# Transposing the probabilities of a windowed attention 128 rows at a time

## The chip, the cores and the metric

The kernel runs on one core of one Trainium2 chip. The metric is the time of one execution on the device in microseconds (us), and the figure given for a kernel is the median of its runs.

## The reference

Two parts follow each other: an attention with a local window and block summaries, and a gated network without a nonlinearity.

```python
# q, k, v: 4 batches, 8 heads, 768 positions, 64 channels
k_sum = k.reshape(B, H, nb, 32, D).max(axis=3)      # nb = 24 blocks of 32
v_sum = v.reshape(B, H, nb, 32, D).mean(axis=3)
scores_l = scale * q @ k^T, kept where |i - j| < 16, else -1e9
scores_s = scale * q @ k_sum^T + log(32)
a = softmax(concat([scores_l, scores_s]))           # with 1e-9 added to the sum
attn = a @ concat([v, v_sum])
x = attn, heads side by side: 3072 tokens x 512
out = ((x @ w1) * (x @ w2)) @ w3 @ w_out            # 512 -> 1024 -> 1024 -> 512
```

## The kernel before

The tokens are cut into six groups of 512, and the heads are taken two at a time, so there are 24 *steps*: a step is one pair of heads for 512 tokens. Each group of 512 tokens is four blocks of 128, and each block has two halves of 64 rows. A half of 64 rows meets 96 positions of its window and 24 summaries, 120 columns in all (`KR`).

A step goes through these stages:

1. `begin` and `scores` (line 355): 32 products of 64 x 64 by 120 columns, for two heads, four blocks and two halves. Each product uses one quarter of TensorE's array: the head decides the rows, the half the columns. The scores of one head lie in one PSUM bank, the two halves of a block one above the other in its 128 partitions.
2. `reduce`, `expose`, `invert` and `normalize` (lines 364 to 402): VectorE adds the mask and takes the maximum, ScalarE takes the exponential and the sum, and the rows are divided by their sums. The probabilities of a step are the tile `sm`, 128 partitions by 8 by 120. The index `j` of the middle counts heads and blocks: `j = 4 * head + block`.
3. `transposes` (line 413): TensorE transposes the probabilities, since the next product needs the 120 columns on the partitions. Each transpose is a product with an identity as the moving operand and the probabilities as the weights. There are two PSUM banks, `tp[0]` and `tp[1]`, one for each half `g`.
4. `evacuate` (lines 418 to 422): one copy of each bank to SBUF, `pt[0]` and `pt[1]`. The first is ScalarE's, the second ScalarE's or VectorE's.
5. `outputs` (line 433): 32 products of 120 x 64 by 64 columns, probabilities times values. The head decides which 64 columns of the array are used.

Between these stages stand the products of the network. Line 123 (`products`) serves the folding of `w3` and `w_out` into one matrix (`w,w`) and the network of the first 1024 tokens (`x,w` and `wp,h`); line 708 (`lanes`) serves the network of the other 2048 tokens (`ln`), in a scheme with seven products in place of eight. Both take 128 x 128 weights and 512 columns, with operands rounded to f32r and split into a high and a low part, three products for one.

The order on TensorE's queue is written out by hand: `tc.manual_schedule` holds for SyncE and TensorE in the first loop, and for TensorE and GpSimd in the second. The first loop counts slots `t`. Steps 0 to 3 begin at slots 12, 18, 20 and 23 (`FIRST`), and the transposes of step `s` stand at slot `FIRST[s + 1]` (`first_pair`). Steps 4 and 5 are transposed together at the last of these slots (`four_pairs`), where step 4 uses the banks `tp` and step 5 the banks `sc` of the scores (`SPARE`). From then on `lump(p)` takes one step at a time: transposes of step `p - 2`, copies, scores of step `p`, eighteen or 24 products, outputs of step `p - 2`, and more products until the count `UP_TO[p]` is reached. For `p` of 24 and 25 there are no scores left, and products follow the transposes at once.

Of the kernel before, what the change touches and what calls it, by code (L numbers as in the profile page):

```python
# [19 lines left out]
P = 128  # L20
# [50 lines left out]
def attention_moe(ctx, tc, qG, kW, kT, vP, vW, vB, mask, w1, w2, w3T, wo, out, outT):  # L71
    nc = tc.nc
# [4 lines left out]
    NBLK = U // P  # L77
# [5 lines left out]
    KR = CUT + NB  # L83
# [16 lines left out]
    ident = const.tile([P, P], F32, name="ident")  # L100
# [305 lines left out]
    def transposes(sm, **more):  # L406

        tp = [ps.tile([P, 512], F32, name="tp", **more or {"bufs": 2}) for _ in range(2)]
        for j in range(NI):
            for g in range(2):  # L410
                rows = slice(64 * g, 64 * g + 64)
                to, p = tp[g][:KR, j * 64 : j * 64 + 64], sm[rows, j]
                nc.tensor.transpose(to, p, ident[rows, rows])  # L413
        return tp

    def evacuate(tp, second="V"):
# [8 lines left out]
    def outputs(pt, v, **more):  # L425

        po = ps.tile([P, 512], F32, name="po", **more or {"tag": "tp", "bufs": 2})
        for i in range(NBLK):
            for g in range(2):
                at = (2 * i + g) * 64  # L430
                for h in range(2):
                    cols = slice(h * D, (h + 1) * D)
                    nc.tensor.matmul(  # L433
                        po[cols, at : at + 64],
                        lhsT=v[:KR, g, i, cols],
                        rhs=pt[g][:, (h * NBLK + i) * 64 : (h * NBLK + i + 1) * 64],
                        start=True,
                        stop=True,
                    )
        return po  # L440
# [583 lines left out]
    def first_pair(s):  # L1024

        u, sm, mx, sc = begin(s)
        yield
        reduce(u, 0, sc, sm, mx)
        reduce(u, 1, sc, sm, mx)
        expose(0, sm, mx)  # L1030
        yield
        expose(1, sm, mx)
        invert(mx)
        yield
        normalize_alone(s, sm, mx)
        while t[0] < FIRST[s + 1]:
            yield
        pt = evacuate(transposes(sms.pop(s)[0], **(SPARE if BANKS[s] == "S" else {})), SECOND[s])
        yield
        keep_x(outputs(pt, values.pop(s)), xs[u])  # L1040
# [15 lines left out]
    def four_pairs(s):  # L1056

        steps = two_pairs(s)
        yield from steps
        while t[0] < FIRST[-1]:  # L1060
            yield
        steps = two_pairs(s + 2)
        tps = [transposes(sms.pop(p)[0], **more) for p, more in zip((s, s + 1), ({}, SPARE))]
        pts = [evacuate(tp, SECOND[p]) for p, tp in zip((s, s + 1), tps)]
        next(steps)
        for p, pt in zip((s, s + 1), pts):
            keep_x(outputs(pt, values.pop(p)), xs[place(p)[0]])
        yield
        yield from steps
# [128 lines left out]
    def finish_step(p, pt, **more):  # L1198
        u, c = place(p)
        po = outputs(pt, values.pop(p), **more)  # L1200
        if u < 2:
            keep_x(po, xs[u])
        else:
            keep_raw(po, u, c)
# [30 lines left out]
    def lump(p):  # L1235
# [8 lines left out]
        with tc.manual_schedule(engines={engines.Activation, engines.DVE}):  # L1244
            tp = transposes(sms.pop(p - 2)[0], **more)
            pt = evacuate(tp, 'V' if p in (12,13,) else 'A')
            b = begin(p) if p < NS else None
            if b:
                u, sm, mx, sc = b
                reduce(u, 0, sc, sm, mx)  # L1250
                if p > NFIRST + 1:
                    expose(0, sm, mx)
                    reduce(u, 1, sc, sm, mx)
# [91 lines left out]
```

## Time and profile before

| | us |
|---|---|
| median of 3 runs | 515.07 |
| lowest and highest run | 512.62 and 517.27 |
| the profiled execution, its own time | 512.96 |
| its span, first to last instruction | 511.2 |
| TensorE busy | 487.7 |
| transposes, union of their times (384 of them) | 16.4 |

Times in the profile are microseconds from the start of the span. PE is a product on TensorE and PEld the load of its weights, DVE is VectorE, ACT ScalarE, POOL GpSimd and SPq the queue of SyncE. A group of instructions is given by line, engine, operation, names (output<-inputs) and shapes; `64*120 64x64` is a product with 64 rows and 120 columns of weights and 64 moving columns. Products overlap in a pipeline, so the duration of one is longer than the distance to the next, and it is the distance between starts that fills the engine. The chain of waits follows the work that ended last back from the end of the span, and gives each piece its start and its length.

### The profile page before, as it was taken

How to read it: one execution, taken by the hardware profiler on the slowest of the kernel's cores; microseconds unless marked ns; L12 is line 12 of the kernel's file. 1: busy time of each engine (PE TensorE's matmuls, PEld its weight loads, DVE VectorE, ACT ScalarE, POOL GpSimd, SP SyncE). 2: the span in 40 equal slices, each digit the busy share in tenths (PEclk: the TensorE clock that was granted, in tenths of full speed). 3: DMA queues.
4: the chain of work that ended last, by engine and by line, in shares of the span. 5: the costliest groups of instructions: out<-in, count | busy, mean ns of one | idle time of the engine just before them, and what ended most of it. 6: DMA issues, size and time to landing. Idle time of an engine off the chain costs nothing.

```text
span 511.2 us, 10373 instructions
## 1 busy us (share of the span) xinstructions
PE 487.7 (95%) x3744; PEld 392.1 (77%) x3744; DVE 365.1 (71%) x883; ACT 314.2 (61%) x879; POOL 46.9 (9%) x86
## 2 busy tenths in 40 slices
PE   0989987999999999999999999999999999999996
PEld 0767766888887877777777887877787888888885
DVE  4979987688833598985459795899978029129972
ACT  5588964468635788878797677657875421423710
POOL 1024433011201210000000000000000000000000
PEclk9999997999999999999999999999999999999999
DMA  8996699999299989889987999998677755655762
GB/s 342 414 375 244 259 305 321 359 398 412 82 286 306 272 283 281 260 254 339 334 302 251 311 311 333 338 327 252 210 247 247 240 179 192 206 174 197 211 200 85
DMA packets 57220, 139.82 MB, mean 274 GB/s; under 512 B 6224, under 2 KB 19024, under 8 KB 54608
## 3 DMA queue, kind: packets, MB, share of 16 engines
q1 hardware_dynamic: 54864, 134.95, 77.5%
q0 software_dynamic: 1152, 2.10, 2.5%
q10 hardware_dynamic: 1152, 2.10, 1.1%
q8 instruction: 30, 0.49, 0.4%
q14 instruction: 22, 0.18, 0.1%
HBM read 106.42 MB, written 32.70 MB: 272 GB/s over the span
## 4 chain that ended last, share of the span: by engine, by line
PE 83%; DVE 5%; DMA 5%; ACT 5%; issue 1%; SPq 0%; ACTq 0%
PE ln L708 46%; PE mm L123 27%; PE po L433 5%; PE sc L355 4%; PE tp L413 2%; DMA rows<-in_vP_dram 2%; ACT sm L383 2%; DVE wf L186 2%; DMA v<-in_vW_dram 2%; DMA wraw<-in_wo_dram 1%; ACT wf L174 1%; ACT w L200 1%; DVE wf L183 1%; DVE w L119 1%; DVE ks L246 1%
## 5 line engine op out<-in xcount | busy, mean ns | idle before, releaser
L708 PE MATMUL ln<-xT,ws 128*128 128x512 f32 x672 | 157.1, 392 | 0.0
L708 PEld LDWEIGHTS ln<-xT,ws 128*128 128x128 f32 x672 | 125.0, 188 | 27.6 <-issue 0.8
L123 PE MATMUL mm<-x,w 128*128 128x512 f32 x384 | 92.5, 399 | 0.0
L123 PEld LDWEIGHTS mm<-x,w 128*128 128x128 f32 x384 | 72.7, 192 | 16.4 <-issue 0.8
L383 ACT ACTIVATE sm<-sm,mx 128x120 f32<-128x120 f32 x192 | 73.9, 389 | 9.3 <-DVE mx L369 9.3
L708 PE MATMUL ln<-hT,ws 128*128 128x512 f32 x336 | 78.3, 392 | 0.0
L728 DVE TENSOR_TENSOR tmp<-ln,tmp 128x512 f32<-128x512 f32 x52 | 35.8, 688 | 56.3 <-PE ln L708 42.1
L708 PEld LDWEIGHTS ln<-hT,ws 128*128 128x128 f32 x336 | 62.6, 188 | 13.4 <-issue 0.2
L123 PE MATMUL mm<-w,w 128*128 128x512 f32 x192 | 50.2, 414 | 14.3 <-ACT w L200 11.9
L619 ACT CAST hT<-hr 128x512 fp32r<-128x512 f32 x56 | 32.1, 622 | 42.6 <-DVE hr L785 35.4
L123 PEld LDWEIGHTS mm<-w,w 128*128 128x128 f32 x192 | 36.8, 197 | 24.7 <-ACT w L200 12.1
L369 DVE CUSTOM_DVE_ANT_0 sm<-sc,mask_sb 128x120 f32<-128x120 f32 x192 | 42.2, 276 | 15.1 <-PE sc L355 15.0
L123 PE MATMUL mm<-wp,h 128*128 128x512 f32 x192 | 46.3, 395 | 0.0
L393 ACT ACTIVATE sm<-sm,mx 128x120 f32<-128x120 f32 x128 | 38.9, 387 | 6.1 <-DVE mx L389 6.1
L123 PEld LDWEIGHTS mm<-wp,h 128*128 128x128 f32 x192 | 35.4, 188 | 8.0 <-issue 0.5
L119 DVE TENSOR_TENSOR hT<-hr,hT 128x512 fp32r<-128x512 f32 x56 | 35.5, 684 | 3.2 <-ACT hT L619 3.0
L383 ACT ACTIVATION_READ_ACCUMULATOR sm<-sm,mx 128x1 f32 x192 | 36.8, 192 | 0.0
L342 POOL COPY k<-ks 128x96 f32<-128x96 f32 (+1 forms) x32 | 12.9, 412 | 218.3 <-DMA k<-in_kW_dram 178.4
L433 PEld LDWEIGHTS po<-pt,v 120*64 120x64 f32 x768 | 25.2, 141 | 9.2 <-issue 5.0
L200 ACT CAST w<-wf 128x1024 fp32r<-128x1024 f32 (+1 forms) x22 | 21.3, 967 | 14.0 <-DVE wf L186 14.0
L433 PE MATMUL po<-pt,v 120*64 120x64 f32 x768 | 28.7, 229 | 1.1 <-DMA v<-in_vW_dram 0.6
L174 ACT ACTIVATE wf<-wraw 128x1024 f32<-128x1024 f32 (+1 forms) x22 | 23.1, 1056 | 8.0 <-DMA wraw<-in_wo_dram 3.6
(60 smaller groups left out, 548.5 us busy)
## 6 DMA issues: line engine op xcount, KB each, us to landing
ws<-wS SPq DMA_DIRECT2D x56, 512.0 KB
wraw<-in_w3T_dram SPq DMA_DIRECT2D x8, 1024.0 KB
wraw<-in_w_dram SPq DMA_DIRECT2D x8, 1024.0 KB
wS<-sp SPq DMA_DIRECT2D x16, 512.0 KB
ws<-pS SPq DMA_DIRECT2D x16, 512.0 KB
k<-in_kW_dram SPq DMA_DIRECT2D x20, 368.0 KB
raw<-in_kT_dram SPq DMA_DIRECT2D x16, 392.0 KB
q<-in_qG_dram SPq DMA_DIRECT2D x24, 256.0 KB
```

Source lines behind the costliest of these rows:

```text
L119: eng.tensor_tensor(dst, src, hi.bitcast(F32), ALU.subtract)
L123: nc.tensor.matmul(acc, lhsT=a, rhs=b, start=first and i == 0, stop=last and i == len(terms) - 1)
L174: nc.scalar.activation(f[:, some], words[:, some, 1].bitcast(F32), AF.Prelu, scale=2.0**-112, alpha=-(2.0**32),)
L200: nc.scalar.copy(t[:, 0, some], f[:, some])
L355: nc.tensor.matmul(sc[h][64 * g : 64 * g + 64, i * KR : (i + 1) * KR], lhsT=q[rows, i * P + 64 * g : i * P + 64 * g + 64], rhs=k[rows, i, ...
L369: nc.vector.tensor_tensor_reduce(out=sm[:, j], in0=sc[h][:, i * KR : (i + 1) * KR], in1=mask_sb[:, 0 if blk == 0 else 2 if blk == BLOCKS - ...
L383: nc.scalar.activation(sm[:, j], sm[:, j], AF.Exp, bias=mx[:, 0, j : j + 1], scale=-1.0, accum_out=mx[:, 1, j : j + 1])
L393: nc.scalar.activation(sm[:, j], sm[:, j], AF.Copy, scale=mx[:, 2, j : j + 1])
L433: nc.tensor.matmul(po[cols, at : at + 64], lhsT=v[:KR, g, i, cols], rhs=pt[g][:, (h * NBLK + i) * 64 : (h * NBLK + i + 1) * 64], start=Tru ...
L619: nc.scalar.copy(dst[0], src)
L708: nc.tensor.matmul(banks[i][:, :U], lhsT=x, rhs=y, start=c + j == 0 and k in o.first, stop=c == steps - 1 and j == 2 and k in o.last, skip ...
L728: nc.vector.tensor_tensor(parts[to], got, parts[more], ALU.add)
```

## The change

In `transposes` the inner loop over the halves `g` goes. One transpose takes all 128 partitions of `sm[:, j]` with the whole 128 x 128 identity as the moving operand, and writes 128 columns. The bank is now chosen by the head (`j // NBLK`) and the place in it by the block. So a bank holds one head with the blocks and halves in order of the tokens, where it held one half with heads and blocks. In `outputs` the moving operand is taken from the bank of the head `h`, at the same place `at` at which the result is written.

```diff
         tp = [ps.tile([P, 512], F32, name="tp", **more or {"bufs": 2}) for _ in range(2)]
         for j in range(NI):
-            for g in range(2):
-                rows = slice(64 * g, 64 * g + 64)
-                to, p = tp[g][:KR, j * 64 : j * 64 + 64], sm[rows, j]
-                nc.tensor.transpose(to, p, ident[rows, rows])
+            nc.tensor.transpose(tp[j // NBLK][:KR, j % NBLK * P : (j % NBLK + 1) * P], sm[:, j], ident)
         return tp
...
                     nc.tensor.matmul(
                         po[cols, at : at + 64],
                         lhsT=v[:KR, g, i, cols],
-                        rhs=pt[g][:, (h * NBLK + i) * 64 : (h * NBLK + i + 1) * 64],
+                        rhs=pt[h][:, at : at + 64],
                         start=True,
                         stop=True,
                     )
```

## The prediction

> **What bounds the kernel now.** I read the page's header first, then busy time by stage, then the chain of waits, and last single bursts of transposes in order of time.
>
> ```profile
> span 511.2 us, 10373 instructions
> ...
> PE 487.7 (95%) x3744; PEld 392.1 (77%) x3744; DVE 365.1 (71%) x883; ACT 314.2 (61%) x879; POOL 46.9 (9%) x86
> ```
>
> TensorE is busy for 95% of the span. The share is an average, so the stages decide (per row: stretch, its length, busy us and count of PE, PEld, DVE, ACT, POOL, then clock, DMA share, GB/s):
>
> ```profile
> 84.00:250.00 166.00, 165.99 (x1432) 133.83 (x1432) 116.52 (x341) 113.56 (x363) 19.18 (x35) 0.99 0.91 297
> 250.00:386.00 136.00, 136.00 (x1176) 108.81 (x1169) 109.42 (x289) 100.35 (x307) 2.30 (x10) 1.00 0.88 290
> ```
>
> From 84 to 386 us TensorE has no gap at all and its clock is full: every nanosecond that its stream grows or shrinks there moves the end. The chain of waits says the same and gives the pieces (start, us, what):
>
> ```profile
> 133.13 1.09 PE tp L413 x32
> 134.21 1.17 PE sc L355 x34
> ...
> 136.43 2.02 PE po L433 x64
> ...
> 146.83 0.20 PE tp L413
> ...
> 156.10 0.61 PE tp L413 x13
> ...
> 202.71 0.61 PE tp L413 x16
> 203.32 0.98 PE sc L355 x32
> 204.30 4.35 PE mm L123 x18
> 208.65 1.08 PE po L433 x32
> ...
> 281.09 8.38 PE ln L708 x36
> ...
> 349.74 0.61 PE tp L413 x16
> ...
> 365.15 0.61 PE tp L413 x16
> 365.76 4.33 PE ln L708 x18
> ...
> 379.55 0.61 PE tp L413 x16
> ...
> 385.57 121.46 PE ln L708 x534
> ```
>
> A step is one pair of heads for 512 tokens; there are 24. Each has one burst of sixteen transposes (line 413), and twenty of these bursts lie on the chain: a double one at 133 (two steps), one split into 1 and 15 at 147 and 156, fifteen from 162 to 350 that stand between products and scores like the one at 202.71, and two at 365 and 380 that stand between products and products. The other four come before 84 us.
>
> **The change, part by part.** It removes 16 transposes of 64 rows a step and adds 8 of 128 rows. No copy, DMA or bank is added, and the SyncE and GpSimd queues are not touched. So the price is the TensorE time of a burst before and after, taken from these rows.
>
> *Spacing now.* Thirty-two transposes take 1.09 us, sixteen 0.61, so eight pairs cost 0.48: 0.060 a pair. The two halves of a pair sit in different rows of the array and run together. That is visible in single slices (count of transposes in flight):
>
> ```profile
> 202.72:202.74 0.02, 0.02 (x2) 1.00 2.00 819
> 202.74:202.76 0.02, 0.02 (x4) 1.00 0.00 0
> ...
> 202.80:202.82 0.02, 0.02 (x6) 1.00 0.50 205
> ```
>
> They arrive by twos. So "half as many instructions" is no halving: sixteen now cost eight time slots.
>
> *What a burst costs besides.* In order of time:
>
> ```profile
> 202.32 0.39 PE L123 MATMUL mm<-x,w 128*128 128x512 f32 x1
> 202.64 0.68 PE L413 MATMUL tp<-ident,sm 64*120 64x64 f32 x16
> ```
>
> From the last product to the first transpose it is 0.32 us, while products follow each other every 121.46/534 = 0.2275. Entering the burst thus costs 0.09. The second pair comes at 202.75, 0.11 behind the first in place of 0.06: 0.05 for a first weight load that nothing covers. Of the burst's 0.61, 0.48 is spacing and 0.05 that load, so 0.08 is for leaving it. Entering products after a burst costs 0.10: 36 of them take 8.38, which is 0.19 over 36 x 0.2275, of which 0.09 is for leaving.
>
> *Spacing of the wide transpose.* No row shows it. Its stream is 128 columns of f32 in place of 64, and it has the array to itself. The nearest rows are these:
>
> ```profile
> L413 PE MATMUL tp<-ident,sm 64*120 64x64 f32 x384 | 16.4, 225 | 1.7 <-POOL sm L402 1.7
> ...
> L280 PE MATMUL means<-rows,mean_sb 128*24 128x128 f32 x48 | 1.5, 274 | 0.0
> ```
>
> ```profile
> 30.95 1.51 PE L280 MATMUL means<-rows,mean_sb 128*24 128x128 f32 x48
> ```
>
> Line 280 streams 128 f32 columns through all 128 rows, four side by side in different columns of the array: 48 take 1.51 us, less the last one's 0.274, over 11 gaps: 0.11 a group of four. That is the lower end. The upper end is today's transpose with its stream doubled, 2 x 0.060 = 0.12: same operation, same 120 columns of weights. I take 0.12, because it is the same operation and because line 280's weights are much narrower. The gain from running two halves at once is exactly what is lost: eight slots of 0.060 become eight of 0.12.
>
> What comes back is the change of shape. Products use 128 rows and 128 columns of the array, the wide transpose the same rows and 120 columns, so I take the 0.09 for entering and the 0.05 of uncovered load as gone. Leaving towards scores (64 x 64) stays at 0.08.
>
> *Sum.* Single step: from the last product to the first score, now 0.32 + 0.61 = 0.93; after, 0.2275 + 8 x 0.12 + 0.08 = 1.27. That is +0.34, fifteen times: +5.1.
> Double step: 0.32 + 1.09 = 1.41 becomes 0.2275 + 16 x 0.12 + 0.08 = 2.23, +0.82. Part of it returns:
>
> ```profile
> 134.73 0.61 ACT L420 COPY pt<-tp 120x512 f32<-120x512 f32 x1
> ...
> 135.39 0.81 PEld L355 LDWEIGHTS sc<-k,q 64*64 64x64 f32 x30 [0.24 <-ACT pt L420]
> ```
>
> The second scores wait 0.24 for the copy that empties their bank. After the change the first of each two banks is full halfway, so three of four copies start before the burst ends and the last needs 0.6 of the 0.98 that the first scores take; the wait goes. +0.58.
> Split step: its lone transpose costs 0.32 + 0.20 + (0.2275 + 0.10) = 0.85 up to the second product, after 0.2275 + 0.12 + 0.2275 = 0.58: -0.27. The other seven: 0.2275 + 7 x 0.12 + 0.08 - 0.93 = +0.22. Together -0.05.
> The two late steps: 0.32 + 0.61 + 0.10 = 1.03 becomes 0.2275 + 0.96 = 1.19, +0.16 each, +0.3.
> Total 5.1 + 0.58 - 0.05 + 0.3 = +5.9, say 6.0 us. With 0.11 a transpose, 160 of them on the chain take 1.6 less: +4.4.
>
> *Parts costed at nothing.* The four early steps lie where other work ends last:
>
> ```profile
> 74.37 8.38 DMA v<-in_vW_dram
> ```
>
> ```profile
> 76.92 0.69 PE L413 MATMUL tp<-ident,sm 64*120 64x64 f32 x16 [1.72 <-POOL sm L402]
> ...
> 81.09 0.64 PE L355 MATMUL sc<-k,q 64*64 64x120 f32 x16 [2.09 <-POOL k L342]
> ```
>
> The chain reaches 82.7 through VectorE, ScalarE and this load, and TensorE idles 2.09 us for a GpSimd copy behind the last of the four bursts. Without that cover they cost 4 x 0.34 = 1.4. The outputs now need the first copy for one head and the second for the other, so their first product needs both. Behind them stand 0.98 of scores and 4.35 of products, against two copies of 0.6: nobody waits. No wait is added.
>
> The profiled execution took 512.96 us with its span of 511.2; the runs shown have their median at 515.07. I add the 6.0 to the median: 521.
>
> **A rule against the sum.** Line 280 moves 128 f32 columns in 0.11 us, while products of 512 columns come every 0.2275: a quarter of the columns in half the time, so plain f32 costs about two passes. The Trainium skill, "FP8 and Floating Point Precision", section "TensorE Precision Notes", says that true FP32 takes four passes, by which the sum would be the third rival's, 538; the row speaks against four.
>
> **The rivals.**
>
> *The array is emptied anyway* (0.22). The products are rounded f32 and the transposes plain f32 in a transposing mode; if that change of mode, and not the tile, costs the 0.09, 0.05 and 0.10, they stay. Every change of shape around the products is also one of type, so the rows can't exclude it. Single: 0.32 + 0.05 + 0.96 + 0.08 = 1.41, +0.48, x15 = 7.2; double 2.37 - 1.41 - 0.24 = +0.7; split about +0.4; late +0.48 each. +9.3: 524.4. [...]
>
> *The weights set the pace* (0.12), the other side. If 0.060 is the load of 120 columns and not the stream of 64, a wide transpose with the same 120 also takes 0.060. Then a single step is 0.2275 + 0.48 + 0.08 = 0.79, -0.14, x15 = -2.1; double -0.14 - 0.24; split -0.5; late -0.33 each. -3.6: 511.5, no slower. The point from which it decides: a single step breaks even at (0.93 - 0.31)/8 = 0.077 a transpose. Against it: outputs stream 64 columns too, with 64 columns of weights, and 32 more of them, sixteen pairs, cost 2.02 - 1.08 = 0.94, 0.059 a pair. With half the weights the pace is the same.
>
> *Four passes when the array isn't shared* (0.05). Then 128 columns stand like a product's 512, 0.2275 a transpose: 160 x 0.1075 = 17 more, +23: 538. For it: every f32 row is of a shared array. Against: 0.11 for four of line 280 together.
>
> *Nothing reaches the end* (0.03), because TensorE's stretch has slack that the rows hide: 515. Against: 165.99 of 166.00.
>
> **How the numbers follow.** The forecast holds 0.58: +4.4 to +6.0, 519.5 to 521. About 1% (5.2 us) is what can be told from no change here. Of the forecast's 0.58 some 0.4 lies above it, since 0.12 is likelier than 0.11; with 0.22 and 0.05 this is 0.66 for slower. Within 1%: the rest of the forecast 0.17, the weights 0.11, nothing 0.03: 0.31. Faster by over 1% needs -5.2, past the second rival's sum: 0.03. The range takes in forecast and first rival and leaves out the weights and the four passes: 517 (519.5 less the 2 us by which the runs shown differ from their median) to 527.
>
> **What would show it.** Line 413 with 192 transposes of 128x128; eight filling about 0.96 us of starts; bursts on the chain of about 1.0; 0.23 from the last product to the first transpose (0.32 would be the first rival); spacing 0.06 the second, 0.23 the third; no wait for the copy L420 at the double step; the same 0.2275 in the last stretch. I am wrong if the spacing of eight is under 0.08, or if a new wait stands ahead of scores or outputs.

## The result

The changed kernel takes 518.92 us (median; 516.57 to 524.41) against 514.58 for the kernel before on the same occasions: a ratio of 1.008, 95% interval 1.0055 to 1.0104. That is slower by 4.3 us: less than the 1% that the prediction took as the bound of what can be told apart, but the interval is clear of 1. The ratio leaves out the one slow run, 524.41. The profiled execution took 518.46 us with a span of 516.7.

The profile after, its header and busy time:

```profile
span 516.7 us, 9978 instructions
...
PE 492.6 (95%) x3552; PEld 400.9 (78%) x3552; DVE 365.7 (71%) x883; ACT 313.9 (61%) x879; POOL 44.7 (9%) x86
```

192 TensorE instructions fewer, and 4.9 us more of TensorE. The group of the transposes, and the one wait of TensorE that the profile has between 86 and 391 us:

```profile
L410 PE MATMUL tp<-ident,sm 128*120 128x128 f32 x192 | 24.8, 272 | 0.0
```

```profile
PE ln L705 <- DVE xT L119: 0.8, 1, 0.8
```

The chain of waits of the changed kernel (start, us, what), beside the rows shown of before:

```profile
133.69 1.75 PE tp L410 x16
135.44 1.80 PE sc L355 x64
137.24 2.02 PE po L430 x64
...
204.24 0.87 PE tp L410 x8
205.11 0.98 PE sc L355 x32
206.09 4.30 PE mm L123 x18
210.40 1.08 PE po L430 x32
...
370.49 0.88 PE tp L410 x8
371.36 4.11 PE ln L705 x18
...
391.00 121.41 PE ln L705 x534
```

A single step's burst went from 0.61 to 0.87. At the double step the burst went from 1.09 to 1.75, and the scores behind it from 1.17 + 1.04 = 2.21 to 1.80. The last stretch of products is as it was. The spacing shows in slices of 20 ns (count of transposes in flight):

```profile
204.08:204.10 0.02, 0.02 (x1) 1.00 0.17 26
204.18:204.20 0.02, 0.02 (x2) 1.00 1.01 205
204.28:204.30 0.02, 0.02 (x3) 1.00 0.33 51
```

One arrives at a time, where two did. The trace's starts are 0.108 to 0.110 apart in every burst, the first gap included, and the first transpose of a burst starts 0.230 after the last product where it was 0.319.

One thing that the kernel's description ahead of the prediction has wrong: scores and outputs are sixteen products a step in the code, not 32. The profile records two instructions for each. That matters below.

### The profile page after: what moved, and what is told of

Its sections match the earlier page's. It is cut to its first block, busy times and chain, and to the rows that moved or that the text cites. A ratio compares the mean times of both kernels' runs of the same rounds, so it can differ in the third digit from the quotient of the medians.

```text
span 516.7 us, 9978 instructions
## 1 busy us (share of the span) xinstructions
PE 492.6 (95%) x3552; PEld 400.9 (78%) x3552; DVE 365.7 (71%) x883; ACT 313.9 (61%) x879; POOL 44.7 (9%) x86
## 4 chain that ended last, share of the span: by engine, by line
PE 80%; DVE 9%; DMA 6%; ACT 2%; issue 1%; SPq 1%; ACTq 0%
PE ln L705 43%; PE mm L123 26%; PE po L430 4%; PE sc L355 3%; PE tp L410 3%; DMA rows<-in_vP_dram 2%; DVE wf L186 2%; DMA v<-in_vW_dram 2%; DVE w L119 2%; DVE sm L369 1%; DMA wraw<-in_wo_dram 1%; DMA wS<-sp 1%; DVE wf L183 1%; DVE wp L119 1%; DVE ks L246 1%
## 5 line engine op out<-in xcount | busy, mean ns | idle before, releaser
L355 PE MATMUL sc<-k,q 64*64 64x120 f32 x768 | 25.2, 270 | 4.5 <-POOL k L342 4.5
```

The source lines that it names most:

```text
L355: nc.tensor.matmul(sc[h][64 * g : 64 * g + 64, i * KR : (i + 1) * KR], lhsT=q[rows, i * P + 64 * g : i * P + 64 * g + 64], rhs=k[rows, i, ...
```

## The experiments

Each is a kernel of its own, timed against the kernel before on the same chip unless said otherwise.

**Every wide burst twice.**

```diff
-        for j in range(NI):
+        for j in (*range(NI), *range(NI)):
             nc.tensor.transpose(tp[j // NBLK][:KR, j % NBLK * P : (j % NBLK + 1) * P], sm[:, j], ident)
```

> Every burst of eight wide transposes is issued twice (the second writes the same places again). Theory: TensorE's stream is the bound from 84 us on and each wide transpose costs 0.109 us there: 160 more on the chain add 17.4 us to the changed kernel's 518.9, 536.3 us, ratio to before 1.042, and a burst that stands between products and scores takes 15 x 0.109 = 1.64 us from first to last start. Rival: part of a burst is hidden behind other work's waits: under 530 us, ratio under 1.03.

Measured: 534.74 us, ratio 1.0403 (1.0365 to 1.0441). The chain:

```profile
197.80 1.75 PE tp L410 x16
199.55 0.98 PE sc L355 x32
...
210.90 1.75 PE tp L410 x16
```

Each burst grew from 0.87 to 1.75, so eight more cost 0.88, which is 0.11 each; the starts in the trace stand 0.109 apart. The stretch from the last outputs ahead of the long products to the last outputs of all took 321.6 us, 15.8 more than the changed kernel's 305.8, and the medians differ by 15.8 as well. Most of the 1.6 that is missing from the expected 17.4 stands in the two traces: a stall of 0.84 that is gone, and three products fewer at half clock, 0.2 each. So a transpose more lengthens this stretch by nearly its whole spacing.

**Ordinary products in place of the transposing mode.**

```diff
-            nc.tensor.transpose(tp[j // NBLK][:KR, j % NBLK * P : (j % NBLK + 1) * P], sm[:, j], ident)
+            to = tp[j // NBLK][:KR, j % NBLK * P : (j % NBLK + 1) * P]
+            nc.tensor.matmul(to, lhsT=sm[:, j], rhs=ident, start=True, stop=True)
```

> The wide transposes are issued as ordinary f32 products with the identity, no transposing mode; shapes and count are those of the changed kernel. Theory: the stream of 128 f32 columns sets the spacing of 0.109 and the mode has no part in it: 0.11 again, the entry stays at 0.23, and the time at 518 to 520 us, ratio to before 1.007 to 1.010. Rival: the ordinary load of 120 columns (0.1 us, as the first two loads of a product run stand 0.107 apart) can't be covered by a stream as short as it is: 0.2 a transpose, 160 x 0.09 = 14 us more, 533 us, ratio 1.036.

Measured: 533.34 us, ratio 1.0363 (1.0328 to 1.0399). The time is the rival's, the reason is neither. The groups by shape (count, busy us, mean ns):

```profile
L411 PE MATMUL tp<-ident,sm 128*120 128x128 f32 x384 | 45.9, 273 | 0.0
```

The code asks for 192 products and the profile has 384 instructions. Their starts stand 0.109 apart, from the first gap of a burst on, and each product takes two of them. An ordinary f32 product of 128 columns costs 0.218, the transposing mode half of that.

**The same with 64 moving columns at a time.**

```diff
-            nc.tensor.transpose(tp[j // NBLK][:KR, j % NBLK * P : (j % NBLK + 1) * P], sm[:, j], ident)
+            for g in range(2):
+                at = j % NBLK * P + 64 * g
+                to = tp[j // NBLK][:KR, at : at + 64]
+                nc.tensor.matmul(to, lhsT=sm[:, j], rhs=ident[:, 64 * g : 64 * g + 64], start=True, stop=True)
```

> Sixteen ordinary f32 products a step with 128 rows and 120 columns of weights and 64 moving columns, so the stream of each is half as long and each set of weights is loaded twice. Theory: if the stream sets the pace even at 64 columns, 0.055 to 0.06 each, 320 on the chain are 320 x 0.058 - 160 x 0.109 = +1.1 us on the changed kernel: 520 us, ratio 1.010. Rival: the load sets a floor of about 0.1: 320 x 0.105 - 17.4 = +16 us, 535 us, ratio 1.040.

Measured: 567.66 us, ratio 1.1039 (1.1001 to 1.1077).

```profile
205.78 3.31 PE tp L413 x32
209.09 0.98 PE sc L355 x32
```

Thirty-two instructions a burst, since each product is two, at 0.105: 640 more of them on the chain than the changed kernel's 160 make up 640 x 0.105 - 160 x 0.109 = 49.8, and the medians differ by 48.7. With half the stream the spacing hardly fell, from 0.109 to 0.105. The trace tells why: the first gap of a burst is 0.055, the others 0.103 to 0.105, and behind the second one the loads of the weights stand as far apart. The first two loads start with the product ahead of the burst and with the first transpose. So 64 columns take 0.055 where the weights are there in time, and otherwise the ordinary load of 120 columns sets a floor of 0.105. The expectation's rival had that floor, and missed the doubling. By the 0.055, an estimate for 128 columns is 0.11: the 0.109 of the ordinary products above is then the stream, though it lies close to the floor of the load. The transposing mode does not show that floor: the kernel before loads 120 columns of two row halves every 0.059.

**Wide transposes of rounded operands.** Results of the mask addition, the exponential and the division are written as f32r, so the probabilities lose low bits. Of the edit, the identity and the transposes are shown.

```diff
-    ident = const.tile([P, P], F32, name="ident")
+    ident = const.tile([P, P], F32R, name="ident")
...
-            nc.tensor.transpose(tp[j // NBLK][:KR, j % NBLK * P : (j % NBLK + 1) * P], sm[:, j], ident)
+            to = tp[j // NBLK][:KR, j % NBLK * P : (j % NBLK + 1) * P]
+            nc.tensor.transpose(to.bitcast(F32R), sm[:, j].bitcast(F32R), ident)
```

> The wide transposes take f32r operands: the mask addition, the exponential and the division round their results in sm to f32r, which changes the probabilities in their low bits; the shapes and the count are those of the changed kernel. Theory: the spacing of 0.109 is the stream of 128 plain f32 columns at two passes; f32r takes one (512 columns in 0.2275, so 128 in 0.057 or a little more): spacing 0.06, 160 x 0.049 = 7.8 us less than the changed kernel, 511.1 us, ratio to before 0.993, faster than both. Rival: the load of 120 columns of weights sets the pace, about 0.1 us as the first two loads of a product run stand 0.107 apart: spacing stays at 0.10 to 0.11 and the time at 518 to 519, ratio 1.007 to 1.009.

Measured: 515.04 us, ratio 1.0019 (0.9994 to 1.0043): between the theory and its rival.

```profile
L413 PE MATMUL tp<-ident,sm 128*120 128x128 f32 x192 | 18.6, 240 | 1.4 <-POOL sm L404 1.4
```

```profile
201.13 0.61 PE tp L413 x8
201.74 0.98 PE sc L357 x32
```

The same shape at the same clock fills 18.6 us where plain f32 filled 24.8, so plain f32 is what sets 0.109. That it is the stream and not the load shows at the first gap of a burst: the second load starts with the first transpose in both kernels, and the gap is 0.108 with plain f32 and 0.059 with f32r. But the spacing fell to 0.06 only at first: the starts of the burst at 201 us are 59, 61, 88, 76, 78, 80 and 86 ns apart, 75 on average. The trace has the loads of the weights 79 to 84 ns apart behind the second one. So the stream takes the expected 0.06 where the weights are there in time, and then the transposes follow the loads; why a load takes 0.08 here was not separated. A burst then costs what two narrow halves cost, 0.61. The prediction's point of break-even, 0.077 a transpose, is tried here: at 0.075 the time can't be told from that of the kernel before. The profiled execution has 2.0 us of waits of TensorE for ScalarE after 356 us, so the time bears this out only roughly.

**Only the early steps, only the late steps.** The wide transposes and their layout are used for steps 0 to 3 alone, or for steps 4 to 23 alone. `WIDE(s)` says whether step `s` is one of them; `outputs` chooses its operand by the same test.

```diff
         for j in range(NI):
-            nc.tensor.transpose(tp[j // NBLK][:KR, j % NBLK * P : (j % NBLK + 1) * P], sm[:, j], ident)
+            if WIDE(s):
+                nc.tensor.transpose(tp[j // NBLK][:KR, j % NBLK * P : (j % NBLK + 1) * P], sm[:, j], ident)
+            else:
+                for g in range(2):
+                    rows = slice(64 * g, 64 * g + 64)
+                    nc.tensor.transpose(tp[g][:KR, j * 64 : j * 64 + 64], sm[rows, j], ident[rows, rows])
```

> Only steps 0 to 3 transpose 128 rows at a time; steps 4 to 23 keep the row halves. Theory: the four early bursts lie under VectorE, ScalarE and the load of v, and cost the end nothing: 514.6 us, ratio 1.000 within 0.002, and the last outputs ahead of the long product stretch start at 82.8 us as before. Rival: the 0.7 us by which that place was later in the changed kernel's profile (83.55 for 82.83) is the early bursts' doing, since ScalarE's and VectorE's order there is planned anew: 515.3 us, ratio 1.0014, and the place at 83.5.

Measured: 516.72 us, ratio 1.0051 (1.0023 to 1.008).

> Only steps 4 to 23 transpose 128 rows at a time; steps 0 to 3 keep the row halves. Theory: the whole cost is here, 160 transposes at 0.109 us in place of 160 pairs at 0.059, less what the entries give back: +4.4 us, 519.0 us, ratio 1.0085, and from the outputs at 82.8 us on every piece as in the changed kernel. Rival: part of the cost is the early steps', and this one gains 0.7 us on the changed kernel: 518.2, ratio 1.007.

Measured: 516.57 us, ratio 1.0032 (1.0003 to 1.0061).

Neither theory. By the ratios the early four cost 2.6 us and the late twenty 1.6, less than their TensorE time, with intervals that overlap. The traces don't bear the first out: in the early kernel's trace the last outputs ahead of the long stretch start at 84.5, between the kernel before's 84.3 and the changed kernel's 85.0. So two more profiles were taken.

**Both kernels again.**

> The kernel before again, for a second profile of it. Theory of a late stall: TensorE's stretch from 86 to 386 us, without a gap in the profile shown, has gaps of 1 to 2 us in other executions, because ScalarE and VectorE behind it are near their limit, and a longer TensorE stream takes these up; this profile then shows such gaps. Rival: the stretch is always full and the profile shows none, and what differs between executions lies before 86 us and in the slices of half clock there. Either way the ratio is 1.000 within 0.003.

> The changed kernel again, on the same chip as the other runs of this study: ratio 1.008 within 0.003, and from the last outputs before the long product stretch to the last outputs of all 303.5 to 304 us when slow clock and gaps are taken off, 3.6 to 4.0 more than the kernel before.

Measured: 515.12 us, ratio 0.999 (0.9958 to 1.0022), and 518.64 us, ratio 1.0085 (1.0057 to 1.0113). TensorE's waits in the late stretch of the kernel before's second profile (in all, times, longest):

```profile
PE po L433 <- ACT pt L418: 0.9, 2, 0.5
PE ln L708 <- DVE xT L119: 0.4, 1, 0.4
PE ln L708 <- DVE tmp L728: 0.2, 1, 0.2
PE po L433 <- ACT pt L420: 0.2, 1, 0.2
```

The first profile has none. So the stretch that the prediction read as always full is full in some executions. In this one TensorE waits near 256 and 266 us for copies of ScalarE, 1.1 us by these rows, and near 274 and 276 us for VectorE, 0.6; shorter gaps bring the sum to 1.9. The chain behind the first of them:

```profile
244.10 10.38 DMA q<-in_qG_dram
...
254.49 0.02 ACTq L532
...
254.55 0.34 ACTq L532
```

Line 532 is the store of an output tile, issued from ScalarE's own queue. ScalarE is idle for 3.69 us there, and the profile puts that down to a load of `q` that landed 10.38 us after its issue; why the store waits for it the profile doesn't say. What ScalarE has to do behind the store, the copies of the transposes among it, starts late. In the first profile the same store goes out while ScalarE is still busy.

**A filler that keeps the clock up.** In the first profiles of both kernels TensorE idles before 82 us, and the clock granted then is half for 6.8 us, in which the first products of the long stretch fall. Twelve products of the identity with itself, overwritten later, were put where the scores of step 5 wait.

```diff
         for i in range(NBLK):
+            for _ in range(filler if i == 2 else 0):
+                nc.tensor.matmul(sc[1][:, 2 * KR : 2 * KR + P], lhsT=ident, rhs=ident, start=True, stop=True)
...
-        return u, sm, mx, scores(*inputs.pop(s))
+        return u, sm, mx, scores(*inputs.pop(s), 12 if s == 5 else 0)
```

> The kernel before, with twelve products of the identity with itself, whose result is overwritten, at the place near 79 us where TensorE waits for a GpSimd copy. Theory: that idle time ends in 3.4 to 10.2 us of half clock from about 82 us on, which costs the first products of the long stretch 0.2 us each; filling it keeps the clock up: 1.0 to 1.5 us less, 513.5 us, ratio 0.9975, slow clock per run down by half or more, and less spread. Rival: the wait behind it sets the end and the clock is beside the point, or the filler delays the scores: 514.9 to 515.5, ratio 1.000 to 1.001.

> The changed kernel with the same twelve products at the same place, where its idle time was 3.3 and 4.5 us in its two profiles. Theory: 1.0 to 2.0 us less than the changed kernel, 517.3 us, ratio to before 1.005; the distance to the kernel before with the filler is then the cost on TensorE's stream alone, 2.9 to 4.1. Rival, as with the kernel before: 518.9, ratio 1.008.

> Only steps 4 to 23 transpose 128 rows at a time, with the filler. Theory: with the clock kept up the early bursts make no difference, so this equals the changed kernel with the filler within 0.7 us: 517.3, ratio 1.005. Rival: the early bursts cost 1.7 to 2.6 us by themselves, as the runs with only the early or only the late steps changed gave: 515.2, ratio 1.001.

> Only steps 0 to 3 transpose 128 rows at a time, with the filler. Theory: equals the kernel before with the filler within 0.7 us: 513.5, ratio 0.9975. Rival: 1.7 to 2.6 us above that one: 515.5, ratio 1.0015.

| with the filler | median us | ratio to before |
|---|---|---|
| kernel before | 512.81 | 0.9998 (0.9972 to 1.0023) |
| changed kernel | 517.01 | 1.0051 (1.0022 to 1.0080) |
| only late steps wide | 515.93 | 1.0011 (0.9983 to 1.0039) |
| only early steps wide | 515.43 | 1.0000 (0.9967 to 1.0033) |

In the kernel before, the clock did what was expected. By stretch (length, TensorE busy and count, clock, DMA share, GB/s), first the kernel before, then the same with the filler:

```profile
82.00:89.00 7.00, 6.65 (x43) 0.51 1.04 317
89.00:96.00 7.00, 7.00 (x32) 1.00 1.04 315
```

```profile
78.00:82.00 4.00, 4.00 (x69) 0.57 1.03 281
82.00:89.00 7.00, 7.00 (x83) 1.00 1.04 333
```

The half clock falls into the filler. In the changed kernel's profile it does not: TensorE still waits 2.95 us ahead of the last early outputs, and 3.4 us of half clock follow from 84.0. Over the executions of that occasion the mean granted clock of the kernel before is 0.992, of the same with the filler 0.997. The medians of that pair differ by 1.5 us, but the interval of the ratio holds 1, so a faster version is not shown. The distance of the two kernels with the filler is 517.01 - 512.81 = 4.2 by the medians, as without it, but 2.7 by the ratios: whether the clock is a part of the change's cost is not settled. The split stays open too. By the medians with the filler the early steps are worth 2.6 or 1.1 (only early against none, all against only late), the late ones 3.1 or 1.6; by the ratios the early ones 0.1 or 2.1, the late ones 0.7 or 2.6. Of the four theories only the changed kernel's came by both measures, and the run with only the late steps changed is at its rival's ratio.

The ten profiles of these kernels say more on the late part. From the last outputs ahead of the long products to the last outputs of all, less the 0.2 by which each product at half clock is longer, the stretch took (in the last of the row halves fourteen instructions of `outputs` ran at half clock too, and are not taken off):

| steps 4 to 23 | us | waits of TensorE in it |
|---|---|---|
| row halves: before, again, early only, filler, early only with filler | 298.9, 302.0, 301.0, 298.9, 303.1 | 0.0, 1.9, 1.1, 0.0, 2.7 |
| wide: after, again, late only, filler, late only with filler | 303.8, 304.3, 303.0, 302.9, 303.3 | 0.8, 1.2, 0.0, 0.0, 0.4 |

Without waits the wide transposes cost 302.9 - 298.9 = 4.0. But the row halves wait more, up to 2.7, and the mean of the five is 300.8 against 303.5: 2.7. It looks as if part of the added TensorE time took the place of waits for ScalarE and VectorE that some executions of the row halves have. With five executions each, two of the row halves and two of the wide ones without a wait, that is not shown. Why the runs with only the early steps changed are slower than this leaves room for was not settled.

## Why the prediction was right, and where not

It was right in its sign, its range and its mechanism, 521.0 forecast for 518.92. Its largest chance, slower by over 1%, did not come: 0.8% is in the case that was given 0.31.

- *"Half as many instructions is no halving."* Holds. Two halves ran side by side at 0.059 a pair, one wide one takes 0.109.
- *Spacing of 0.12.* This is the term that was mis-sized. It was taken over 0.11 because the operation was the same; measured 0.109, and 160 x 0.011 = 1.8 us is most of the distance between the sum, +5.9, and what the two kernels with the filler show for steps 4 to 23: +3.8 by the starts from the double step on, +4.0 by the table above. That the sum's lower end, +4.4, is so near the 4.3 of the medians is in part luck: the medians also hold waits and whatever the early steps cost, and the sum lacks 0.6 that the products gave back.
- *The reason for 0.11.* Right by luck. Line 280's 48 instructions are 24 products, each recorded twice, so the "group of four" in 0.11 was four half products. The row seemed to agree because a transpose is one such instruction. The prediction also argued from it that plain f32 costs two passes. The run with ordinary products decides otherwise: 0.218 for 128 columns, where products of 512 f32r columns stand 0.2275 apart, 0.057 for 128. That is 3.8 times as long. The Trainium skill, "FP8 and Floating Point Precision", section "TensorE Precision Notes", gives four passes for true FP32, and the trace agrees with its 3.8. The transposing mode takes half of that, 0.109, which the prediction has nowhere.
- *What comes back.* The 0.09 for entering went (0.319 to 0.230), the 0.05 of the first load went (0.108 from the first gap on), leaving stayed: 0.203 less the last transpose's 0.109 is 0.094, before 0.150 less 0.059 is 0.091. So going from f32r products to full-height f32 transposes empties nothing, 0.230 for the products' own 0.2275, and the first rival falls. The Trainium skill, "TensorEngine Tiling (Array Packing)", "Key Properties", says that a change of the tiling mode drains TensorE; the trace agrees, with 0.319 where the transposes take 64 rows of the array.
- *The sum, step by step.* Single steps +0.26 for +0.34. The double step: +0.66 in the burst and -0.41 in the scores (2.21 to 1.80), +0.25 for +0.58; the wait for the copy went as forecast, and with it more than its 0.24. The late two +0.05 for +0.16, by 0.88 + 4.11 against 0.61 + 4.33. The split step +0.03 for -0.05: its lone transpose gave back 0.13 where 0.27 was forecast. Not foreseen: the runs of 18 products behind the scores fell from 4.35 to 4.30, 0.6 in all; the cause stays open.
- *"No gap at all."* True of the profile shown and not of the kernel: the second profile has 1.9 us of gaps. One execution was read as a rule. "Its clock is full" does not hold for the start of the stretch even there: the clock was half until 89.0 us, which the mean of 0.99 hides.
- *The early steps at nothing.* Not settled. The prediction did not think of a new order on ScalarE and VectorE there: the chain ahead of 83 us runs mostly through ScalarE in the first profile of the kernel before and mostly through VectorE in that of the changed one. TensorE's wait for GpSimd's copy of `k` was 2.1 and 0.7 us in the two profiles of the kernel before, 4.5 and 3.3 in those of the changed one.
- *The other rivals.* Weights that set the pace: there is such a floor, 0.105, in ordinary products, and loads 0.08 apart hold up the f32r transposes; but the wide transpose of plain f32 took 0.109 and not 0.06. Four passes when the array isn't shared: 0.109 and not 0.2275. Nothing reaches the end: every burst twice added 15.8 us.

## What to carry to other kernels

Before halving a count of small TensorE instructions, look at whether they run side by side: here two in different rows of the array shared a time slot of 0.059, and the one of full height with twice the stream took 0.109. What a full-height form gives back is the change of array shape, here 0.09 at the entry and 0.05 for the first load, against 0.05 more for each transpose, so in plain f32 it would pay only in bursts of one or two (an estimate from these numbers). At 0.075 a transpose the two could not be told apart. And count a row's instructions against the calls in the code before a spacing is read from it.

## What was not expected of the hardware

An ordinary f32 product is two TensorE instructions here (384 for 192 calls, 0.109 each at 128 columns), and the transposing mode one.

A load of weights was seen to set the pace in two forms: 0.105 apart for ordinary f32 products with 120 columns of weights, 0.08 for f32r transposes with as many.

The granted clock falls to half behind idle time of TensorE, in pieces of 3.41 us: in the kernel before's two profiles for 6.8 us from 82.1 and for 10.2 us from 78.0, in the run with only the late steps changed for 3.4, twice. A product then takes 0.427 in place of 0.227. The Trainium skill, "TensorE: Matmul & The Clock Gate", Part 1, gives a free-running window of 3.4 us and half rate after an idle one. The traces agree on the length and the half rate, but TensorE was not idle for a whole window: of the 3.41 us ahead of such a stretch it stood idle for 1.55 to 3.12. Executions of the kernel before lie between 510.7 and 519.3 us, and a lower mean clock goes with a longer time (correlation -0.65 over 35 of them). That the clock makes the difference is not shown: with the filler, at a mean of 0.997, no faster kernel was.
